# Issuing one of two small output stores from SyncE instead of ScalarE, one weight piece earlier, at the end of a two-cache attention decode kernel

## Chip, cores and metric

One Trainium2 chip; the kernel runs on one core. The metric is the device time in microseconds (us). All executions quoted here are in the same, undisturbed state ("fast"). "Span" is the time from the first to the last instruction in the profile of one execution. It is about 1.2 us shorter than the device time.

Some terms. SyncE, ScalarE (ACT in the views), VectorE (DVE) and TensorE (PE) are engines of the core. SyncE or ScalarE issues a transfer with one instruction, the "issue"; the 16 DMA engines then carry it out in packets. A load brings data from the chip's main memory to the core's, a store takes data back to it. A semaphore is a counter by which one engine, or a transfer that is complete ("has landed"), releases another engine that waits. The cast is VectorE's copy of a block's result into `orow`, from which it is stored.

## The reference

Two independent attention blocks, A and B, with the same shapes. Each does one decode step over a long cache. The output is the two results side by side.

```python
B, Sq, D = 8, 1, 1024;  H, Sk, Dh = 32, 4096, 128          # all bf16
def ref(x, k_cache, v_cache, wq, wo):
    q = (x @ wq).reshape(B, Sq, H, Dh).transpose(0, 2, 1, 3)
    scores = jnp.einsum("bhqd,bhkd->bhqk", q, k_cache) * Dh ** -0.5
    p = jax.nn.softmax(scores, axis=-1)
    o = jnp.einsum("bhqk,bhkd->bhqd", p, v_cache)
    return o.transpose(0, 2, 1, 3).reshape(B, Sq, H * Dh) @ wo
return concatenate([ref(A...), ref(B...)], axis=-1)         # 8 x 1 x 2048
```

## The kernel before

Large loads (8 MB tiles of K, V, wq and wo) go through a ring of three buffers. All of them are issued by SyncE. Only the end matters here. The last load is block B's wo, 8 MB. It is issued as four pieces, each with its own semaphore, so that the projection can begin before all of it is there.

```python
wo_cuts = ((0, 20), (20, H - 4), (H - 4, H - 1), (H - 1, H))     # 5120, 2048, 768, 256 KB
...                                                   # cut: set-up, attention loop
def make_proj(c):                                     # c = 0: block A, c = 1: block B
    w = tile_of("wo", c)
    for i, (r0, r1) in enumerate(wo_cuts if c == NC - 1 else ((0, H),)):
        ...                                           # cut: 4 x (r1 - r0) matmuls into proj
        opProj[c] = add("pe", emit, [opNorm[c], opT[("wo", c, i)], c_pad, opEv.get(c - 1)])
    opEv[c] = add("dve", lambda e: e.tensor_copy(orow[:, c, :], proj[:, 0:DT]), [opProj[c]])
    outs.append(dma(out[:, 0, c * D:(c + 1) * D].rearrange("b (q n) -> q b n", q=NT), orow[0:128:32 // B, c, :],
                    ("out", 0), [opEv[c]] if c == NC - 1 else [opEv[c], opT[("wo", NC - 1, len(wo_cuts) - 1)]],
                    "sp" if c == NC - 1 else "act"))
...
nc.sync.wait_ge(sems[("out", 0)], counts[("out", 0)])   # the program's last instruction: SyncE waits for both stores
```

Each store writes 16 KB as 4 groups of 8 rows of 512 bytes. Below, "A" is the store of block A's output and "B" that of block B's. "The third piece" of wo is the last but one and "the last piece" is the fourth.

Of the kernel before, what the change touches and what calls it, by code (L numbers as in the profile page):

```python
# [31 lines left out]
class _Program:  # L32
# [11 lines left out]
    def add(self, eng, emit, deps=(), dma_key=None, moves=False):  # L44
        op = _Op(eng, emit, list(deps), dma_key, moves)
        if dma_key is not None:
            self.counts[dma_key] = self.counts.get(dma_key, 0) + 16
            op.token = (dma_key, self.counts[dma_key])
        for d in op.deps:
            if not (d.eng == "pe" and eng == "pe"):  # L50
                d.sig = True
        self.ops[eng].append(op)
        return op
# [86 lines left out]
def _build_kernel(nc, caches, out):  # L140
    B, Sq, D = caches[0][0].shape
    _, H, Sk, Dh = caches[0][1].shape
    NC = len(caches)
# [18 lines left out]
    with es:  # L162
# [35 lines left out]
        wo_cuts = ((0, 20), (20, H - 4), (H - 4, H - 1), (H - 1, H))  # L198
# [8 lines left out]
        def dma(out_ap, in_ap, key, deps, eng="sp"):  # L207
            return add(eng, lambda e: e.dma_start(out_ap, in_ap), deps, dma_key=key)
# [22 lines left out]
        opT, opMul, opEacc, opRed, opNgm, opExp = {}, {}, {}, {}, {}, {}  # L231
        opPV, opAcc, opExt, opSt, opQb, opQbc, opQ, opQs, opQT = {}, {}, {}, {}, {}, {}, {}, {}, {}
        opOc, opNorm, opProj, opUse, opPM, opEv = {}, {}, {}, {}, {}, {}
# [20 lines left out]
        def tile_of(kind, n):  # L254
            return ring[:, slot[(kind, n)], :]
# [167 lines left out]
        def make_proj(c):  # L423
            w = tile_of("wo", c)

            for i, (r0, r1) in enumerate(wo_cuts if c == NC - 1 else ((0, H),)):
                def emit(e, r0=r0, r1=r1):
                    for r in range(r0, r1):
                        for q in range(NT):
                            col = r * D + q * DT  # L430
                            x = e.matmul(proj[32 * q:32 * (q + 1), 0:DT], on_sb[:, c, r:r + H * B:HQ],  # L431
                                         w[:, col:col + DT], start=(r == 0), stop=(r == H - 1), tile_position=(0, 32 * q))
                    return x
                opProj[c] = add("pe", emit, [opNorm[c], opT[("wo", c, i)], c_pad, opEv.get(c - 1)])
            opEv[c] = add("dve", lambda e: e.tensor_copy(orow[:, c, :], proj[:, 0:DT]), [opProj[c]])  # L435
            outs.append(dma(out[:, 0, c * D:(c + 1) * D].rearrange("b (q n) -> q b n", q=NT), orow[0:128:32 // B, c, :],
                            ("out", 0), [opEv[c]] if c == NC - 1 else [opEv[c], opT[("wo", NC - 1, len(wo_cuts) - 1)]],
                            "sp" if c == NC - 1 else "act"))


        x_sb = ring[0:B, 2, 0:NC * D].rearrange("p (c d) -> p c d", c=NC)
# [55 lines left out]
        make_ext(n)  # L497
        make_norm(1)
        make_proj(0)
        make_proj(1)  # L500
        assert issued[0] == len(plan)

# [64 lines left out]
```

## Time and profile before

Before: median 2563.64 us (2563.62 to 2563.99).

The page of the kernel before, first: the busy share of the DMA engines in the 40 slices of the span, in tenths, and their total; the two queues (packets, MB, share of the DMA engines' time); and the summary, by engine, of the chain of work that ended last.

```profile
DMA  9999999999999999999999999999999999999999
...
DMA packets 19554, 1107.51 MB, mean 432 GB/s; under 512 B 2184, under 2 KB 2248, under 8 KB 2520
...
q1 hardware_dynamic: 19476, 1107.32, 99.9%
...
q10 hardware_dynamic: 68, 0.05, 0.0%
...
DMA 52%; DVE 28%; issue 16%; PE 4%; ACT 0%; another core or an unknown queue 0%; DVEq 0%; SPq 0%
```

The reader should see that the DMA engines are nine tenths busy or more in every slice. They move 432 GB/s on average, and the packets of queue q1, which is SyncE's, take 99.9% of their time. The stream of weights and caches therefore sets the span. Queue q10 is ScalarE's; it carries the two small x loads and store A.

The chain of waits over the last 48 us (start, length, what), from the last piece of wo on:

```profile
2520.46 39.30 DMA ring<-in_B_wo_dram
2559.75 0.04 issue
2559.80 0.36 PE proj L431 x4
2560.16 0.03 issue
2560.19 0.42 DVE orow L435
```

The timeline of the end (start, length, engine, line, operation; in brackets the idle time before it and what ended it). "SPq" and "ACTq" are the instruction queues of SyncE and ScalarE; a store's line shows its issue only, not its landing.

```profile
2546.85 0.42 DVE L435 CAST orow<-proj 128x256 bf16<-128x256 f32 x1 [14.49 <-PE proj L431]
...
2559.80 0.15 PEld L431 LDWEIGHTS proj<-ring,on_sb 128*32 128x32 bf16 x4 [0.31 <-DMA ring<-in_B_wo_dram]
2559.84 0.65 ACTq L208 DMA_DIRECT2D out_dram<-orow  x1
2560.19 0.42 DVE L435 CAST orow<-proj 128x256 bf16<-128x256 f32 x1 [12.91 <-PE proj L431]
2560.64 0.69 SPq L208 DMA_DIRECT2D out_dram<-orow  x1
```

The longest of SyncE's own waits in the last 63 us (who waited for what: total us, times, longest):

```profile
SPq L208 <- DVE orow L435: 39.7, 1, 39.7
```

Read together: A's row of results was ready at 2547.3. ScalarE issued A at 2559.84, when the last piece of wo had landed. B can only be issued after the last four matmuls and the cast, at 2560.64. Between its last wo issue and that moment SyncE does nothing for 39.7 us. The store's flight is in none of these lines. The trace's records of DMA packets and semaphore arrivals give it:

| kernel before, us from the start of the span | A (ScalarE) | B (SyncE) |
|---|---|---|
| issue begins | 2559.836 | 2560.640 |
| issue takes | 0.652 | 0.688 |
| first packet | 2561.124 | 2561.924 |
| last completion | 2561.712 | 2562.522 |

wo's third piece was complete at 2559.126 and its last piece at 2559.754. The span ends at 2562.555. A is complete 0.81 us before B, so A is not on the chain that ends the span.

### The profile page before, as it was taken

Reading aid. Unit: us, or ns where it says so; the run is one execution under the profiler, and the core shown is the slowest. Engines: PE = TensorE matmul, PEld = TensorE weight load, DVE = VectorE, ACT = ScalarE, POOL = GpSimd, SP = SyncE. Lnnn points to the kernel's source line nnn. Section 1 sums busy time; section 2 is a strip of 40 time slices with the busy share of each in tenths; the row PEclk is TensorE's granted clock in tenths of the full one; section 3 lists DMA queues with packets and bytes.
Section 4 is the critical chain, followed back from the end, with each engine's and each line's share of the span. In section 5 each row is a group of like instructions: output and inputs, shape, how many; then the busy total and the mean of one; then the engine's idle time right before and its main releaser. Section 6 shows DMA issues by size and latency. Waiting matters only on the chain.

```text
span 2562.6 us, 18832 instructions
## 1 busy us (share of the span) xinstructions
PE 1118.0 (44%) x7712; PEld 397.3 (16%) x7712; DVE 2170.6 (85%) x1042; ACT 129.8 (5%) x401; POOL 2.6 (0%) x15
## 2 busy tenths in 40 slices
PE   2443443443444444444434444444444434434435
PEld 0111111111111111111111111111111111111112
DVE  3898898898898898898898888988988988988983
ACT  1100000000000000000000000000000000000000
POOL 0000000000000000000000000000000000000000
PEclk8767676766767766766767666766757666666657
DMA  9999999999999999999999999999999999999999
GB/s 425 427 438 430 436 432 436 432 436 432 436 432 436 430 437 430 436 432 435 432 435 431 435 433 433 435 433 435 432 436 432 435 433 435 433 435 433 435 433 394
DMA packets 19554, 1107.51 MB, mean 432 GB/s; under 512 B 2184, under 2 KB 2248, under 8 KB 2520
## 3 DMA queue, kind: packets, MB, share of 16 engines
q1 hardware_dynamic: 19476, 1107.32, 99.9%
q8 instruction: 7, 0.11, 0.0%
q10 hardware_dynamic: 68, 0.05, 0.0%
q14 instruction: 3, 0.02, 0.0%
HBM read 1107.33 MB, written 0.03 MB: 432 GB/s over the span
## 4 chain that ended last, share of the span: by engine, by line
DMA 52%; DVE 28%; issue 16%; PE 4%; ACT 0%; another core or an unknown queue 0%; DVEq 0%; SPq 0%
DMA ring<-in_A_k_cache_dram 25%; DMA ring<-in_B_k_cache_dram 25%; DVE ring L330 10%; DVE ring L335 10%; PE red L345 4%; DVE s_sb L353 4%; DVE PM L370 3%; DMA ring<-in_B_wo_dram 2%; DVE rmax L359 1%; DVE rtmp L360 0%; ACT PM L291 0%; PE o L285 0%; DVEq L135 0%; DVE ngm L363 0%
## 5 line engine op out<-in xcount | busy, mean ns | idle before, releaser
L330 DVE TENSOR_TENSOR ring<-ring,qbc 128x8192 bf16<-128x8192 bf16 x256 | 1131.8, 4421 | 309.7 <-DMA ring<-in_B_k_cache_dram 152.9
L345 PE MATMUL red<-ring,ident 128*128 128x512 bf16 x2048 | 782.6, 552 | 1391.7 <-DVE ring L335 1391.7
L335 DVE TENSOR_TENSOR ring<-ring 128x4096 bf16<-128x4096 bf16 x256 | 582.2, 2274 | 0.0
L345 PEld LDWEIGHTS red<-ring,ident 128*128 128x128 bf16 x2048 | 239.1, 127 | 1843.5 <-DVE ring L335 1494.1
L353 DVE TENSOR_REDUCE s_sb<-red 128x64 f32<-128x1024 f32 x256 | 311.9, 1218 | 3.5 <-PE red L345 3.5
L382 PE MATMUL pv<-ring,PM 128*32 128x512 bf16 x4096 | 273.3, 414 | 4.7 <-DVE PM L370 4.7
L370 DVE TENSOR_TENSOR PM<-pe,own_h 128x2048 bf16<-128x2048 bf16 x64 | 146.2, 2285 | 0.7 <-ACT pe L365 0.7
L382 PEld LDWEIGHTS pv<-ring,PM 128*32 128x32 bf16 x4096 | 103.6, 103 | 187.4 <-issue 114.3
L319 ACT ACTIVATE qbc<-misc 128x128 bf16<-128x128 f32 x64 | 17.7, 277 | 1091.7 <-PE misc L317 1091.7
L365 ACT ACTIVATE pe<-s_sb,ngm 128x256 bf16<-128x256 f32 x64 | 32.5, 508 | 466.7 <-DVE ngm L363 466.7
L390 ACT ACTIVATE accS<-pv 128x512 bf16<-128x512 f32 x64 | 38.2, 597 | 352.9 <-PE pv L382 352.9
L399 PEld LDWEIGHTS o<-accS,E 128*32 128x32 bf16 x1024 | 31.3, 100 | 49.6 <-issue 48.4
L399 PE MATMUL o<-accS,E 128*32 128x32 bf16 x1024 | 38.1, 185 | 0.7 <-ACT accS L390 0.7
L405 ACT ACTIVATE o_sb<-o 32x32 f32 (+1 forms) x64 | 11.8, 185 | 452.4 <-PE o L399 444.5
L359 DVE TENSOR_REDUCE rmax<-s_sb 128x1 f32<-128x256 f32 x64 | 26.9, 420 | 2.2
L435 DVE CAST orow<-proj 128x256 bf16<-128x256 f32 x2 | 0.8, 424 | 27.4 <-PE proj L431 27.4
L431 PE MATMUL proj<-ring,on_sb 128*32 128x256 bf16 x256 | 12.7, 377 | 15.8 <-DMA ring<-in_A_wo_dram 8.7
L305 DVE COPY qT<-misc 128x64 bf16<-128x64 bf16 x8 | 3.5, 435 | 18.6 <-PE misc L301 18.6
L312 ACT ACTIVATE qst<-qT 128x128 bf16 (+1 forms) x64 | 18.7, 293 | 1.9 <-DVE qT L305 1.9
L360 DVE TENSOR_SCALAR rtmp<-half,rmax 128x32 f32<-128x32 f32 x64 | 15.4, 241 | 2.3
L363 DVE TRANSPOSE_TENSOR_REDUCE ngm<-rtmp 128x1 f32<-128x32 f32 x64 | 13.6, 212 | 2.2
L317 PE MATMUL misc<-ident,qst 128*128 128x128 bf16 x64 | 14.7, 230 | 0.9 <-ACT qst L312 0.9
(33 smaller groups left out, 66.1 us busy)
## 6 DMA issues: line engine op xcount, KB each, us to landing
ring<-in_B_wo_dram SPq DMA_DIRECT2D x1, 5120.0 KB, 33.2
ring<-in_B_wo_dram SPq DMA_DIRECT2D x1, 2048.0 KB, 37.8
ring<-in_B_wo_dram SPq DMA_DIRECT2D x1, 768.0 KB, 39.1
ring<-in_A_k_cache_dram SPq DMA_DIRECT2D x32, 39.9
ring<-in_A_v_cache_dram SPq DMA_DIRECT2D x32, 27.8
ring<-in_B_k_cache_dram SPq DMA_DIRECT2D x32, 39.8
ring<-in_B_v_cache_dram SPq DMA_DIRECT2D x32, 27.8
ring<-in_B_wo_dram SPq DMA_DIRECT2D x1, 256.0 KB, 39.3
```

What stands on the lines that cost most here:

```text
L312: return e.activation(qst[:, n % 2, :].rearrange("p (j m) -> p j m", m=MP), from_.unsqueeze(2).to_broadcast([128, HQ, MP]), ACTF.Copy)
L319: opQbc[n] = add("act", lambda e: e.activation(qbc[:, n % 2, :], misc[:, 0:Dh], ACTF.Copy), [opQb[n], _at(opMul, NR * (n - 2) + NR - 1)])
L330: opMul[s] = add("dve", lambda e: e.tensor_tensor(v, v, qbc[:, n % 2, :].unsqueeze(1).to_broadcast([128, CT, Dh]), ALU.mult), [opT[("k", n ...
L335: return add("dve", lambda e: e.tensor_tensor(v[:, :, 0:64], v[:, :, 0:64], v[:, :, 64:128], ALU.add), [opMul[s]])
L345: i = e.matmul(dst, ident[:], v[:, g, :, j, :], start=(j == 0), stop=(j == 3))
L353: opRed[s] = add("dve", lambda e: e.tensor_reduce(s_sb[:, n % 2, r * CT:(r + 1) * CT], red_ps[s % 2][:, :].rearrange("p (t w) -> p t w", w ...
L359: m = add("dve", lambda e: e.tensor_reduce(rmax[:], s_sb[:, n % 2, :], AX.X, ALU.max), [opRed[NR * n + NR - 1]])
L365: opExp[n] = add("act", lambda e, at: e.activation(pe[:], s_sb[:, n % 2, :], ACTF.Exp, bias=ngm[:, n % 2:n % 2 + 1], scale=scale, accum_ou ...
L370: opPM[n] = add("dve", lambda e: e.tensor_tensor(PM[:], pe[:].unsqueeze(2).to_broadcast([128, T, HQ]), own_h[:].unsqueeze(1).to_broadcast( ...
L382: i = e.matmul(pv_ps[32 * q:32 * (q + 1), :], PM[:, t:t + 4, :].rearrange("p t j -> p (t j)"), v[:, t * Dh:(t + 4) * Dh], start=(g == 0), ...
L390: opAcc[n] = add("act", lambda e: e.activation(accS[:], pv_ps[:], ACTF.Copy), [opPV[n], _at(opExt, n - 1)])
L399: x = e.matmul(to, E[:, i, PH - 1 - u:PH - 1 - u + MB], accS[:, i * 128 + H * u:i * 128 + H * (u + 1)], start=(i == 0 and u == 0), stop=(i ...
```

## The change

The intent: take A off ScalarE and send it a little earlier, once all of wo but the last piece is there, so that it is out of the way when B is to go.

```diff
             outs.append(dma(out[:, 0, c * D:(c + 1) * D].rearrange("b (q n) -> q b n", q=NT), orow[0:128:32 // B, c, :],
-                            ("out", 0), [opEv[c]] if c == NC - 1 else [opEv[c], opT[("wo", NC - 1, len(wo_cuts) - 1)]],
-                            "sp" if c == NC - 1 else "act"))
+                            ("out", 0), [opEv[c]] if c == NC - 1 else [opEv[c], opT[("wo", NC - 1, len(wo_cuts) - 2)]], "sp"))
```

It has two parts: the engine (ScalarE to SyncE) and the wait (last piece to third piece). Nothing else differs.

## The prediction

> **What bounds the kernel.** The page shows DMA at nine tenths or more in all 40 slices, 432 GB/s; DVE is busy 85%, PE 44%. The chain of waits that ended last is 52% DMA. So the stream on SyncE's queue sets the span; the change touches only the last 4 us.
>
> **The tail, from the timeline and the trace's DMA packets and landings (us from the span's start).** The four wo pieces are issued by SyncE at 2519.14 to 2520.46. Their semaphores are full at 2552.36, 2557.27, 2559.13 and 2559.75; the last piece's last packet ends at 2559.33. orow of the first cache has been ready since 2547.27. Before: ScalarE wakes on the last piece and issues output A at 2559.84 (0.65 us); its packets start at 2561.12 and land by 2561.71. The last projection matmuls run 2559.80 to 2560.16, the cast (DVE) 2560.19 to 2560.61, SyncE issues output B at 2560.64 (0.69 us); its packets start at 2561.92, 1.28 us after the issue began, and land at 2562.52. SyncE's last wait ends there. So the chain that ends the span is: last wo piece, matmuls 0.36, cast 0.42, output B 1.88 us from issue to landing. Output A lands 0.8 us before B: it is off the chain.
>
> **What the change does.** Same transfers. Output A's issue moves to SyncE and wakes on the third piece, at about 2559.13 plus 0.08 (as ScalarE took from its landing to its issue): 2559.21, instead of 2559.84. At 0.69 us it occupies SyncE to about 2559.90. SyncE next needs to be free at 2560.62, when the cast's semaphore arrives: about 0.7 us to spare, so B's issue is not delayed. A's packets should start about 2559.21 + 1.28 = 2560.5, which is 1.2 us after the last wo packet, so they cannot delay the last piece though they now share its queue. A should land near 2561.1.
>
> The Trainium skill (DMA: Bandwidth & Descriptors, "Issuing engines are not separate DMA queues") says that issuing from several engines only saves the sequencer's time; here the time saved before (0.69 us) fitted into a gap of SyncE, so giving it up costs nothing. The same page ("Latency and other measured facts") gives about 600 ns to first byte; the trace agrees: 0.60 us from the end of B's issue to its first packet.
>
> Small things on the chain: B is now the second store on SyncE, and its issue might be shorter than 0.69 us (ScalarE's two x loads took 0.60 and 0.29 us) or slightly longer (back-to-back wo issues took 0.43 against 0.33 us). That is at most about 0.3 us either way; I expect 0.1 us of gain.
>
> **Predicted time:** 2563.5 us, range 2562.2 to 2565.0 (three runs before span 0.35 us; the rest is for drift between sessions). Faster by over 2%: 0.005; within 2%: 0.99; slower: 0.005.
>
> **What would show it.** Right: both stores on SyncE, A issued 2559.1 to 2559.3 on the scale of before, some 0.6 us ahead of the last matmuls; the last piece's landing, matmuls, cast and B's issue at the same distances from one another; the span's end 1.9 us after B's issue.
>
> **What would make it wrong.** A's issue on SyncE taking over 1.4 us and delaying B; A's descriptors slowing the last piece (its landing more than 0.63 us after the third's); or the changed program shifting the long stream's timing by a microsecond or more, which this reasoning does not cover.

## The result, and the profile after

After: median 2563.42 us of six runs (2563.35 to 2563.65); before 2563.64 us. The ratio of the times is 0.9999 with a 95% interval of 0.9986 to 1.0012. A ratio is the mean time of one kernel's fast runs over that of the other's fast runs of the same rounds, so it is not quite the ratio of the medians quoted. The interval reaches about 3.3 us to each side, so a difference of 0.2 us is far inside it. What follows rests on the traces, where the distances at the end repeat to about 0.01 us.

The page after, the same lines:

```profile
DMA  9999999999999999999999999999999999999999
...
DMA packets 19554, 1107.51 MB, mean 432 GB/s; under 512 B 2184, under 2 KB 2248, under 8 KB 2520
...
q1 hardware_dynamic: 19512, 1107.34, 99.9%
...
q10 hardware_dynamic: 32, 0.03, 0.0%
...
DMA 52%; DVE 28%; issue 16%; PE 4%; ACT 0%; another core or an unknown queue 0%; DVEq 0%; SPq 0%
```

The stream is the same. A's 36 packets (32 of data, 4 of completion) moved from q10 to q1.

The chain of waits, the same part of it:

```profile
2519.89 39.72 DMA ring<-in_B_wo_dram
2559.62 0.04 issue
2559.66 0.36 PE proj L431 x4
2560.03 0.02 issue
2560.05 0.42 DVE orow L435
```

The timeline of the end; the line with "x2" is both stores, from the first one's begin to the second one's end:

```profile
2545.67 0.42 DVE L435 CAST orow<-proj 128x256 bf16<-128x256 f32 x1 [14.70 <-PE proj L431]
...
2559.07 1.97 SPq L208 DMA_DIRECT2D out_dram<-orow  x2
2559.66 0.15 PEld L431 LDWEIGHTS proj<-ring,on_sb 128*32 128x32 bf16 x4 [0.32 <-DMA ring<-in_B_wo_dram]
2560.05 0.42 DVE L435 CAST orow<-proj 128x256 bf16<-128x256 f32 x1 [13.95 <-PE proj L431]
```

SyncE's own waits in the last 63 us, the same part of them. A's wait on wo is line L100, the helper that emits waits:

```profile
SPq L100 <- DMA ring<-in_B_wo_dram: 38.7, 1, 38.7
...
SPq L208 <- DVE orow L435: 0.7, 1, 0.7
```

The two stores by the tile that they read (duration in ns: shortest, median, longest):

```profile
L208 SPq DMA_DIRECT2D out_dram<-orow x2: 540/616/691, 2559.1 to 2560.5; - x2
```

The long one is A's, the first; the short one is B's. SyncE's long idle time is now cut in two: 38.7 us until the third piece, then A's issue, then 0.7 us of waiting for the cast. So A's issue fits in with room to spare. The chain is the same chain. One thing did move on it: B's issue took 0.54 us, where it took 0.69 before.

| us | before | after |
|---|---|---|
| last piece of wo complete, from the start of the span | 2559.754 | 2559.617 |
| from there to the end of B's cast | 0.859 | 0.855 |
| from the cast's end to B's issue | 0.027 | 0.028 |
| B's issue takes | 0.688 | 0.540 |
| from B's issue to its first packet | 1.284 | 1.173 |
| from B's issue to its last completion | 1.882 | 1.771 |
| last piece complete to end of span | 2.801 | 2.688 |

The profiled spans differ by 0.25 us (2562.555 and 2562.305). 0.137 us of that was there when the last piece of wo landed, 0.113 us comes after it. The first part is most likely not the change's. The kernels below that leave A on ScalarE and start it at another time have the last piece at 2559.60 and 2559.63, as early as the changed kernel, and in all kernels below it comes between 2559.43 and 2559.69; the one profile of before was late. The second part, 0.11 us, is what the experiments ask about.

### The profile page after: what moved, and what is told of

The parts are those of the page before. It is cut to its first block, busy times and chain, and to the rows that moved or that the text cites. A ratio compares the mean times of both kernels' runs of the same rounds, so it can differ in the third digit from the quotient of the medians.

```text
span 2562.3 us, 18832 instructions
## 1 busy us (share of the span) xinstructions
PE 1115.7 (44%) x7712; PEld 396.7 (15%) x7712; DVE 2170.6 (85%) x1042; ACT 129.9 (5%) x401; POOL 2.6 (0%) x15
## 4 chain that ended last, share of the span: by engine, by line
DMA 52%; DVE 28%; issue 16%; PE 4%; ACT 0%; another core or an unknown queue 0%; DVEq 0%; SPq 0%
DMA ring<-in_A_k_cache_dram 25%; DMA ring<-in_B_k_cache_dram 25%; DVE ring L330 10%; DVE ring L335 10%; PE red L345 4%; DVE s_sb L353 4%; DVE PM L370 3%; DMA ring<-in_B_wo_dram 2%; DVE rmax L359 1%; DVE rtmp L360 0%; ACT PM L291 0%; DVEq L135 0%; DVE ngm L363 0%; PE o L285 0%
## 5 line engine op out<-in xcount | busy, mean ns | idle before, releaser
L363 DVE TRANSPOSE_TENSOR_REDUCE ngm<-rtmp 128x1 f32<-128x32 f32 x64 | 13.5, 211 | 2.2
```

## The experiments

The explanations that were tested for B's shorter issue:

- **First store.** The first store that an engine issues takes longer than a later one. In the changed kernel A is SyncE's first store, so B is its second.
- **Overlap.** Before, B's issue was long because the chip was still busy with A's store, issued by the other engine 0.80 us earlier. The Trainium skill gives this a footing: "Perfetto Trace Analysis", section "DMA Instruction — HWDGE (DVE, Sync)", says that the block that generates descriptors is shared and that an issue's profiled time includes the wait for its lock. The trace of before makes this footing weak: A's issue had ended at 2560.488, 0.15 us before B's began.
- **Switch.** It is not the first store, but a store issued just after loads, that is long.

Ten kernels ran, eight in 5 rounds and two in 3. All gave correct results, and each is "same" against before: the 95% intervals reach 0.13 to 0.17% (3.3 to 4.4 us) to each side. Times before are those of the same chip and rounds. Kernels are compared only within the same rounds. The verdicts rest on these distances; each is from one profiled execution.

| kernel | A: engine, released by | B's issue takes | to its first packet | last piece complete to end of span | median us (before) |
|---|---|---|---|---|---|
| before | ScalarE, last piece | 0.688 | 1.284 | 2.801 | 2563.64 |
| after | SyncE, third piece | 0.540 | 1.173 | 2.688 | 2563.42 (2563.64) |
| e1_sync_last | SyncE, last piece | 0.541 | 1.173 | 2.685 | 2563.55 (2563.61) |
| e2_scalar_third | ScalarE, third piece | 0.695 | 1.292 | 2.807 | 2563.58 (2563.61) |
| e3_sync_nowait | SyncE, own cast | 0.540 | 1.178 | 2.695 | 2563.57 (2563.61) |
| e4_scalar_nowait | ScalarE, own cast | 0.696 | 1.293 | 2.807 | 2563.53 (2563.61) |
| a1_change_again | as after | 0.540 | 1.172 | 2.688 | 2563.57 (2563.65) |
| e5_sync_lastcast | SyncE, B's cast | 0.541 | 1.172 | 3.425 | 2564.30 (2563.65) |
| e6_load_between | SyncE, third piece, then a load | 0.557 | 1.192 | 2.711 | 2563.50 (2563.65) |
| e7_halves | both, third piece, in halves | 0.515 and 0.522 | 1.153 and 1.424 | 2.898 | 2563.76 (2563.65) |
| e8_both_scalar | ScalarE, third piece, B on ScalarE too | 0.548 | 1.184 | 2.704 | 2563.54 (2563.64) |
| e9_forms | SyncE, third piece, in halves | 0.556 | 1.194 | 2.698 | 2563.52 (2563.64) |

The diffs below are against the changed kernel and shortened to the arguments that differ.

### e1_sync_last: the engine alone

```diff
-  [opEv[c], opT[("wo", NC - 1, len(wo_cuts) - 2)]], "sp"
+  [opEv[c], opT[("wo", NC - 1, len(wo_cuts) - 1)]], "sp"
```

> The engine alone: output A on SyncE, but still waiting for the last piece of wo. Repeat theory (the second store issued by SyncE is cheaper than the first): output B's issue takes 0.54 us as after, its first packet starts 1.17 us after the issue began, and the time is that of after, 0.1 us under before; A's issue starts 0.08 to 0.12 us after the last piece's landing, takes 0.69 us and ends just (under 0.1 us) before B's could start, so B may start up to 0.05 us later. Overlap theory (before, B's issue was long because the chip was still working on A's store, issued 0.80 us earlier): B's issue takes 0.69 us or more and its first packet starts 1.28 us after it, the time is that of before.

The two stores in the view by tile (ns):

```profile
L208 SPq DMA_DIRECT2D out_dram<-orow x2: 541/620/699, 2559.7 to 2560.5; - x2
```

B's issue took 0.541 us though A was issued only 0.80 us before it, as in the kernel before. Overlap expected 0.69 us or more. The engine alone gives the whole 0.11 us. A's issue ended at 2560.356 and B's began at 2560.455, 0.027 us after its cast as always, so even with the old wait A was out of the way, by 0.10 us. The time (0.06 us under before by the medians) does not resolve it.

### e2_scalar_third: the wait alone

```diff
-  [opEv[c]] if c == NC - 1 else [opEv[c], opT[("wo", NC - 1, len(wo_cuts) - 2)]], "sp"
+  [opEv[c]] if c == NC - 1 else [opEv[c], opT[("wo", NC - 1, len(wo_cuts) - 2)]], "sp" if c == NC - 1 else "act"
```

> The wait alone: output A stays on ScalarE, but waits for the third piece of wo. Repeat theory: B is SyncE's first store, so its issue takes 0.69 us and its first packet starts 1.28 us after it, the time is that of before within 0.1 us. Overlap theory: A is issued 0.6 us earlier than before, 1.4 us ahead of B as in the changed kernel, so B's issue takes 0.54 us and the time is 0.1 us under before. Both: A's issue begins 0.08 us after the third piece's landing, and the last piece still lands 0.63 us after the third.

```profile
L208 ACTq DMA_DIRECT2D out_dram<-orow x1: 652/652/652, 2559.0 to 2559.0; - x1
L208 SPq DMA_DIRECT2D out_dram<-orow x1: 695/695/695, 2560.5 to 2560.5; - x1
```

B is again SyncE's only store and takes 0.695 us; the distance to the end of the span is that of before. With A 1.43 us ahead of B, overlap expected 0.54. So the earlier wait gives nothing, and overlap has failed twice.

### e3_sync_nowait and e4_scalar_nowait: no wait for wo

```diff
-  [opEv[c]] if c == NC - 1 else [opEv[c], opT[("wo", NC - 1, len(wo_cuts) - 2)]], "sp"
+  [opEv[c]], "sp"                                     # e3
+  [opEv[c]], "sp" if c == NC - 1 else "act"           # e4
```

> No wait for wo at all, A on SyncE: A is issued right after its cast, about 12 us before the end. On the same queue its packets should come behind those of the pieces already queued. Repeat theory: B's issue 0.54 us still, time that of after. Overlap theory: 0.54 us too. If the saving fades with the time between the two stores, B's issue goes back to 0.69 us. The last piece lands at the same distance (0.63 us) from the third; if A's packets get in among wo's, up to 0.25 us later.

> No wait for wo at all, A on ScalarE's own queue, issued right after its cast about 12 us before the end, so that its packets mix with those of wo. Repeat theory: B's issue 0.69 us, first packet 1.28 us after it. Overlap theory: 0.54 and 1.17 us. A's 32 packets take about 0.03 us each, 8 on each of 4 DMA engines, so wo should be held up by 0.0 to 0.25 us; time from 0.1 us under before to 0.3 us over it.

The stores of e3, then those of e4:

```profile
L208 SPq DMA_DIRECT2D out_dram<-orow x2: 540/618/696, 2546.4 to 2560.5; - x2
```

```profile
L208 ACTq DMA_DIRECT2D out_dram<-orow x1: 652/652/652, 2547.0 to 2547.0; - x1
L208 SPq DMA_DIRECT2D out_dram<-orow x1: 696/696/696, 2560.5 to 2560.5; - x1
```

In e3 the two stores are 14 us apart, and B's issue is short all the same: the saving does not fade in that time. In e4 ScalarE's store is 13.5 us ahead of B and complete at 2555.94, 4.6 us before B's issue began, so there can be no overlap, and B's issue is long. This is the clearest refutation of the overlap explanation.

The two runs also show what the wait for wo was worth. In e3 A's packets started 11.2 us after A's issue, at 2557.53, about when the first of the DMA engines was through with the pieces already on the queue (the last piece's first completion came at 2557.70, its last at 2559.63). In e4, on the other queue, they ran from 2550.84 to 2555.29 among those of wo. In both, wo was not delayed by an amount that shows: from the first piece's completion to the last piece's it took 7.399 us (e3) and 7.383 us (e4), against 7.394 before and 7.398 after. So 32 small packets do not need to be held back here at all.

### a1_change_again: the changed kernel once more

> The changed kernel once more, beside the other runs of this call. First-store theory (SyncE's first store costs 0.69 us to issue, a later one of the same shape 0.54 us): A's issue 0.69, B's 0.54 us, first packet of B 1.17 us after its issue began; time within 0.3 us of before, about 0.1 us under it.

It repeats: B's issue 0.540 us, first packet at 1.172, 2.688 us to the end. The medians differ by 0.08 us this time, where they differed by 0.22 before. That is the scatter of these times; a tenth of a microsecond is not to be had from them.

### e5_sync_lastcast: no gap for A's issue, on purpose

```diff
-  outs.append(dma(... out of block c ..., ("out", 0), [opEv[c]] if c == NC - 1 else [opEv[c], <third piece>], "sp"))
+  for c_ in [] if c < NC - 1 else range(NC):          # both stores, A first, once B's cast is done
+      outs.append(dma(... out of block c_ ..., ("out", 0), [opEv[c_], opEv[c]], "sp"))
```

> No slack on purpose: both stores on SyncE and both only after the last cast, A first, B behind it. If the change is free because A's 0.69 us of issue fits into a gap of SyncE, then taking the gap away puts it on the chain: B's issue starts about 0.74 us later after the cast than in the changed kernel, and the time rises by 0.7 us over the changed kernel and by 0.6 us over before. If issues of one engine overlapped, it would rise by less than 0.3 us. First-store theory: A 0.69, B 0.43 to 0.54 us.

The timeline at the end; "x2" is both issues, back to back:

```profile
2560.06 0.42 DVE L435 CAST orow<-proj 128x256 bf16<-128x256 f32 x1 [14.26 <-PE proj L431]
2560.51 1.28 SPq L208 DMA_DIRECT2D out_dram<-orow  x2
```

B's issue began 0.764 us after its cast instead of 0.028, and the time rose by 0.73 us over the changed kernel (2564.30 and 2563.57) and by 0.65 us over before. The two issues, 0.688 and 0.541 us, lay end to end in 1.28 us and did not overlap. This is the cost that the change would have had without SyncE's idle time. It is also the only kernel here all of whose times (2564.20 to 2564.53) lie above all of those of before and of the changed kernel in its call (at most 2563.77). By the interval (0.9989 to 1.0017 of before) even this is "same"; that the 0.7 us is real rests on the 0.736 us later issue in the trace, which the times match.

### e6_load_between: a load between the two stores

```diff
+  spare = sb("spare", [128, 256], BF16)               # and a semaphore ("z", 0)
   outs.append(dma(...))                                # as in the change
+  if c == 0:
+      add("sp", lambda e: e.dma_start(spare[0:B, :], caches[0][0].rearrange("b s d -> b (s d)")[:, 0:256]),
+          [opEv[c], <third piece>], dma_key=("z", 0))
...                                                     # cut: at the program's end SyncE also waits for ("z", 0)
```

> The changed kernel with one small load (8 rows of 512 bytes into spare memory) issued by SyncE between the stores A and B. If the 0.15 us that B saves come from the first store having been done once (first-store theory), B's issue stays at 0.54 us. If they come from the issue just before B being of the same kind, and switching from loads to a store is what costs (switch theory), B's issue goes back to 0.69 us. SyncE is free again before B's semaphore in either case (A 0.69 and the load about 0.3 us within the 1.43 us between A's and B's issue), so B does not start later.

The timeline, with the load, B's cast and B (in this kernel the store's and the cast's lines are one further down):

```profile
2559.86 0.43 SPq L440 DMA_DIRECT2D spare<-in_A_x_dram  x1
2560.09 0.42 DVE L436 CAST orow<-proj 128x256 bf16<-128x256 f32 x1 [13.38 <-PE proj L432]
2560.54 0.56 SPq L209 DMA_DIRECT2D out_dram<-orow  x1
```

B's issue is 0.557 us although the issue just before it was a load. The switch explanation would have it at 0.69, so it fails, as far as so small a load can stand for those of wo. The load's own issue took 0.43 us, not the 0.3 expected, and still fitted in.

### e7_halves: each store cut in two, on both engines at once

```diff
-  outs.append(dma(... 4 groups ..., "sp"))
+  for h, eng in enumerate(("sp", "act")):
+      outs.append(dma(out[:, 0, c * D + h * 2 * DT:c * D + (h + 1) * 2 * DT].rearrange("b (q n) -> q b n", q=2),
+                      orow[64 * h:64 * (h + 1):32 // B, c, :], ("out", 0), gate, eng))
```

> Each output store cut in two halves of 16 rows of 512 bytes, one on SyncE and one on ScalarE at the same time, output A's at the third piece as in the change, so that both engines have stored once before B. An estimate from 0.54 us for 4 groups of 8 rows and 0.29 us for ScalarE's second x load of 1 group of 8 rows: 0.08 us per group, so 0.37 us for a half of 2 groups. B's issue 0.37 us, its first packet about 1.0 us after it, the span 0.15 us under the changed kernel's. If the two engines' issues hinder one another, each takes 0.54 us or more and nothing is gained.

```profile
L208 ACTq DMA_DIRECT2D out_dram<-orow x2: 522/584/647, 2558.9 to 2560.3; - x2
L208 SPq DMA_DIRECT2D out_dram<-orow x2: 515/596/676, 2558.9 to 2560.3; - x2
```

This was a try for a faster tail, and it failed. The estimate of 0.37 us was wrong: half the groups took 0.52 us, nearly as long as all of them. So the time of these issues hardly depends on the number of groups, and dividing the difference between two unlike transfers by their groups had been no way to get at it. Each engine's first store was again the longer one (0.676 and 0.647 us). The two halves of B were issued 0.005 us apart, but their first packets were not: SyncE's came at 1.153 us, ScalarE's at 1.424. The second half therefore completes later than a whole store does, and the distance to the end of the span rises by 0.21 us over the changed kernel; the medians say 0.19. The 0.28 us between the first packets would fit descriptors generated one store at a time, as the Trainium skill has it in the section named under "Overlap". But the lock wait that it puts inside the profiled issue does not show there: both issues are as short as a later store's.

### e8_both_scalar: both stores on ScalarE

```diff
-  ..., "sp"))
+  ..., "act"))
```

> Both stores on ScalarE, A still at the third piece. If the saving goes with being any engine's second store (first-store theory, general), A's issue takes 0.65 us and B's about 0.50 us, and the distance from the last piece's landing to the end of the span is 2.65 to 2.72 us, as with both on SyncE. If it is something of SyncE's alone, B's issue on ScalarE stays at 0.65 us and the distance is 2.8 us or more. The time is within 0.3 us of before.

```profile
L208 ACTq DMA_DIRECT2D out_dram<-orow x2: 548/600/652, 2559.1 to 2560.6; - x2
```

The first takes 0.652 us and the second 0.548 (about 0.50 was expected), with 2.704 us to the end. So it is not SyncE's alone. ScalarE had issued two loads of 8 rows at the start of the program, some 2556 us earlier, and its first store was long nevertheless; SyncE's first store is long 26 to 40 us after its last load of wo. So loads that far back do not do what an earlier store does. No run puts a load just ahead of a first store.

### e9_forms: an earlier store of another form

```diff
-  outs.append(dma(... block A, 4 groups ..., <third piece>, "sp"))
+  for h in range(2):                                  # block A in two halves of 2 groups; block B whole
+      outs.append(dma(... half h, 2 groups ..., <third piece>, "sp"))
```

> All on SyncE, at the third piece; output A in two halves (2 groups of 8 rows of 512 bytes each), output B whole (4 groups), so that B's exact form has not been issued before, but a store has. If any earlier store does, B's issue takes 0.54 us and the distance from the last piece's landing to the end of the span is 2.69 us; if only a store of the same form does, 0.69 us and 2.80 us. The halves take 0.68 and about 0.52 us, so SyncE is free at about 1.3 us after A's start and B does not start later.

```profile
L208 SPq DMA_DIRECT2D out_dram<-orow x3: 516/556/683, 2559.1 to 2560.5; - x3
```

The halves took 0.683 and 0.516 us, and B, of a form not issued before, 0.556. So a store of a different number of groups is enough; the exact form need not have come before.

## Why the prediction was right

- **"... the stream on SyncE's queue sets the span; the change touches only the last 4 us."** Right. The rate is 432 GB/s in both profiles, and the third and last pieces land 0.628 us (before) and 0.630 us (after) apart.
- **"Output A is off the chain."** Right. Issuing A almost 13 us earlier on its old engine (e4) left the distance to the end at 2.807 us (2.801 before).
- **A's issue fits in a gap of SyncE.** Right, and with the numbers given. A's issue began 0.085 us after the third piece was complete (0.08 predicted) and took 0.691 us (0.69 predicted). SyncE then waited 0.7 us for the cast. The counter-test, e5, charges 0.73 us when the gap is gone. The sentence of the Trainium skill that was quoted ("DMA: Bandwidth & Descriptors", section "Issuing engines are not separate DMA queues") holds here: what issuing from a second engine saves is the sequencer's issue time, 0.69 us, and here that time was free.
- **A's packets cannot delay wo.** Right. They started at 2560.36, 1.18 us after the last packet of wo ended. e3 and e4 show that even packets in the midst of wo cost nothing that can be seen.
- **"Small things on the chain ... I expect 0.1 us of gain."** Right in size: 0.113 us in the trace. That the size came out is in part luck: its ground was a weak analogy, ScalarE's two x loads at 0.60 and 0.29 us, and the prediction left open that it might go the other way. Its own mark, the span's end 1.9 us after B's issue, had no room for the gain: it came 1.81 us after it, and 1.92 before. The runs put a cause in its place: here an engine's first store takes 0.65 to 0.70 us to issue, a later one 0.52 to 0.56. Of the 0.148 us saved in B's issue 0.111 arrive at its first packet and at its completion.
- **The skill's figure of about 600 ns to the first byte** ("DMA: Bandwidth & Descriptors", section "Latency and other measured facts") is met if it is counted from the end of an issue to its first packet: 0.60 us for B before, 0.63 us after.
- **What the times show.** The predicted 2563.5 us and the measured 2563.42 us agree, but so would a prediction of no change. In the times this change cannot be told from none. That B saves 0.11 us is shown by the traces (2.685 to 2.711 us to the end in the six kernels in which B is whole, not held back, and a later store of its engine; 2.801 to 2.807 in the three in which it is the first).

What stays open: why a first store is longer. No run looks inside an issue. It is also not known whether a store far earlier than 14 us would still count, nor what a much smaller one would do. So "first" is not told apart from "first after a long pause": every long store began 26 us or more after the end of its engine's issue before it, every short one at most 13.5 us after. Nor is "first store" told apart from "first transfer to this output", for all stores go there. SyncE's loads show neither effect: all 130 in the trace of before that come after a pause of 5.5 to 44.9 us take 0.327 or 0.328 us to issue, the first load of a tensor like the later ones. ScalarE's two x loads at the program's start, 0.60 and then 0.29 us, may show one.

## What to carry to other kernels

Before moving a DMA issue between engines, look at what the receiving engine does at that moment: in a gap the issue is free, next to a critical issue it costs its full length, here 0.7 us. If the last thing a kernel does is a store, let the engine that issues it have issued another store before (up to 14 us before, as far as was tried); that was worth about 0.1 us here, which matters only in kernels far shorter than this one. And judge a change of this size by distances inside the trace, because run-to-run scatter and a late or early stream are larger than it.

## What the Trainium skill lacked or had wrong

- "Perfetto Trace Analysis", section "DMA Instruction — HWDGE (DVE, Sync)": it does not say that an engine's first store can take longer to issue than its later ones. Here 0.676 to 0.699 us and then 0.515 to 0.557 on SyncE, 0.647 to 0.652 and then 0.522 to 0.548 on ScalarE, for stores from 2 groups of 8 rows of 512 bytes to 4.
- The same section puts the wait for the shared descriptor block inside the profiled issue. In e7 two stores issued 0.005 us apart have issues of 0.515 and 0.522 us, no longer than single later stores, but first packets 0.28 us apart. If one waited for the other, it did so after the profiled window.
- "DMA: Bandwidth & Descriptors", section "Latency and other measured facts", does not say from when the 600 ns to the first byte count. Here they fit from the end of the profiled issue (0.60 to 0.63 us for store B before and after), not from its start (1.17 to 1.28 us).
- "DMA: Bandwidth & Descriptors", section "Why a DMA increments its semaphore by 16 and not by 1", has one figure for the sequencer's work on a copy, 512 cycles in "previous generations", and does not say what it depends on. Here it depended on the kind of transfer and its history (loads of wo 0.33 and 0.43 us, stores 0.52 to 0.70 us), and hardly on the number of groups (0.54 us for 4 groups, 0.52 for 2).
